# One-hots by head and operand in the start of an attention kernel, bf16 dummy products, and scaling and roundings moved to GpSimd

## The chip, the cores and the metric

The kernel runs on one core of a Trainium2 chip. The metric is the time of one execution in device microseconds; lower is better. In the text TensorE is the matrix engine (PE in the profile, PEld its weight loads), VectorE is DVE, ScalarE is ACT, GpSimd is POOL and SyncE is SP, whose queue issues the DMAs.

## The reference, cut to what matters

```
q_n, k_n, c_n = q / |q|, k / |k|, centroids / |centroids|
q_assign = argmax_c(q_n . c_n)          # 16 clusters a head
k_assign = argmax_c(k_n . c_n)
scores = where(q_assign == k_assign, q k^T / 8, -1e9)
attn = softmax(scores);  x = attn v      # 2 x 8 heads, 768 rows, width 64
x = leaky_relu(x @ w_in) @ w_out         # 1536 tokens, 512 -> 2048 -> 512
x = relu(x @ w2_in) ** 2 @ w2_out
```

## The kernel before, in words

The 16 heads stand in 8 pairs. A pair's q and k lie transposed in one tile `rqk` (128 partitions: two heads of width 64; `[:, 0]` is q, `[:, 1]` is k). Everything on the attention side is done in fp32 by splitting a number into a rounded part (type fp32r) and the rest: `hb` holds a head's q and k so split, and in 16 more rows of it the one-hots of the clusters, so that one product gives scores and mask together. For a pair that is prepared in the loop, `hi` and `lo` make the split parts in a tile `spl`, and DMAs place them in `hb`. The first pair is not placed by DMA: its q and k are loaded twice into tiles `twice` (SyncE's queue loads `cen`, the first pair's `rqk`, head 0's `twice`, the second pair's `rqk`, head 1's `twice`, then v), `head_hi` writes the rounded parts into `hb`, `head_lo` the rests (L579 for q, L584 for k, both on VectorE with two inputs in SBUF), `mask_mm` transposes the one-hots on TensorE, and `mask_act` writes them into `hb`.

At the start VectorE normalizes the centroids, TensorE transposes them (`ctp`), ScalarE copies them into the block matrix `cbd`, and 12 products (`dots`) give the first pair's dot products with the centroids, of k and then q. `is_max`, `rank`, `first_max` and `one_hot` turn them into one-hots in `pad`, for both heads and both operands at once. `warm_up` runs products of the identity whose result nobody reads.

The loop goes over units of two row tiles (128 rows of scores each); three units make a head. `PLAN` names the steps of a unit in order, each with the number of units by which it lags: S0, S1 scores (`qk_mm`), R0, R1 row maxima (`rowmax`), X0, X1 exponentials (`expo`), RE and RC row sums and reciprocals, N0, N1 normalization on GpSimd (`norm`), Ta to Tc transposes, H and L their rounded part and rest (`eh`, `el`), V the product with v. The order on every engine is the order in which this code is written; no scheduler changes it in this part. For the first units `hooks` hangs further work behind single steps: ("R1", 0) means behind the maximum of the second row tile of unit 0. There the second pair gets its dot products (`dots1`), its cluster maxima (`all_max1`), its ranks and one-hots (`rank`, `first_max`, `one_hot` on GpSimd and VectorE; `oh_trans` transposes them on TensorE), and head 1 gets its one-hots and its rests. GpSimd also splits v (`vlo`).

After the attention the two feed-forward layers follow, in fp32r products with weights split on ScalarE and GpSimd; the change does not touch them.

## Time and profile before

| | |
|---|---|
| time, median of 3 runs | 760.21 us (760.01 to 761.02) |
| time of the profiled execution | 760.79 us |
| its span, first to last instruction | 759.0 us |
| busy: TensorE, VectorE, ScalarE, GpSimd | 98%, 75%, 58%, 51% |
| granted TensorE clock, mean over the span | 0.998 |

A share of busy time is a mean over stages that differ: the start, in which TensorE waits for the other engines, is some 30 of 759 us. The first 30 us are the stretch that the change touches.

### The profile page before, as it was taken

The numbers are of one execution on the slowest core, as the hardware profiler recorded it, in microseconds if no ns is written. First come the engines' busy times: TensorE is split into PE (matmuls) and PEld (weight loads), VectorE is DVE, ScalarE is ACT, GpSimd is POOL, SyncE is SP. The second block draws the span as 40 slices with busy tenths as digits, with TensorE's granted clock in tenths as the row PEclk, the third lists the DMA queues.
The fourth block names the chain that finished last, engine by engine and source line by source line (L and its number), as shares of the span: only waits on it lengthen the run. The fifth ranks groups of instructions, "written<-read, shape, count | busy, mean of one in ns | idle before, by whom it ended". The sixth has DMA issues, their size and how long they took to land.

```text
span 759.0 us, 11071 instructions
## 1 busy us (share of the span) xinstructions
PE 745.1 (98%) x4054; PEld 649.5 (86%) x4054; DVE 570.8 (75%) x860; ACT 443.0 (58%) x816; POOL 387.4 (51%) x345
## 2 busy tenths in 40 slices
PE   8999999999999999999999999998999999999998
PEld 8899999999989888888888888887888888888886
DVE  5999999999999545876666576686568687687755
ACT  6988988988998564345444344556634444443430
POOL 2989889889855326561442414399242441424400
PEclk9999999999999999999999999999999999999999
DMA  7494574562601213111131112211111211122004
GB/s 231 102 220 110 118 172 111 116 173 68 156 21 62 107 56 111 55 56 57 56 111 56 55 56 73 94 57 56 56 57 62 99 62 55 56 76 91 1 1 166
DMA packets 16902, 66.35 MB, mean 87 GB/s; under 512 B 3152, under 2 KB 4048, under 8 KB 11856
## 3 DMA queue, kind: packets, MB, share of 16 engines
q1 hardware_dynamic: 16848, 65.65, 29.2%
q8 instruction: 32, 0.52, 0.3%
q14 instruction: 22, 0.18, 0.1%
HBM read 44.60 MB, written 3.15 MB: 63 GB/s over the span
## 4 chain that ended last, share of the span: by engine, by line
PE 85%; DVE 11%; ACT 3%; issue 1%; POOL 0%; DVEq 0%; POOLq 0%
PE o L847 35%; PE h L770 32%; PE A L487 6%; PE S L389 5%; PE T L452 5%; DVE el L469 4%; DVE nm L412 3%; ACT e L422 2%; ACT eh L463 1%; DVE ds L319 1%; DVE xt L509 1%; PE warm L242 1%; DVE m L318 1%; PE S L297 1%; DVE m L330 0%
## 5 line engine op out<-in xcount | busy, mean ns | idle before, releaser
L134 POOL TENSOR_TENSOR wl<-wt,wh 128x1024 fp32r<-128x1024 f32 x32 | 77.2, 2414 | 132.0 <-ACT wh L133 132.0
L818 DVE TENSOR_TENSOR gl<-h,gh 128x512 fp32r<-128x512 f32 x96 | 65.7, 690 | 69.0 <-ACT h L813 50.3
L770 PE MATMUL h<-xh,wh 128*128 128x512 f32 x288 | 112.0, 391 | 2.1 <-DVE gl L818 2.1
L770 PE MATMUL h<-xl,wh 128*128 128x512 f32 x288 | 112.5, 391 | 0.0
L770 PE MATMUL h<-xh,wl 128*128 128x512 f32 x288 | 112.2, 390 | 0.0
L865 DVE TENSOR_TENSOR acc<-o,acc 128x512 f32<-128x512 f32 x144 | 92.9, 686 | 12.4 <-PE o L847 12.4
L469 DVE TENSOR_TENSOR el<-T,eh 128x512 fp32r<-128x512 f32 x144 | 94.4, 683 | 4.4 <-ACT eh L463 3.2
L439 POOL TENSOR_SCALAR e<-e,r 128x768 f32<-128x768 f32 x96 | 87.6, 924 | 19.4 <-DVE r L436 13.1
L412 DVE TENSOR_REDUCE nm<-S 128x1 f32<-128x768 f32 x96 | 90.8, 947 | 4.2 <-PE S L297 2.4
L422 ACT ACTIVATE e<-S,nm 128x768 f32<-128x768 f32 x96 | 87.2, 909 | 11.1 <-DVE nm L412 6.7
L389 PE MATMUL S<-hb 128*128 128x384 f32 (+1 forms) x384 | 90.2, 349 | 2.0 <-ACT e L422 1.2
L463 ACT CAST eh<-T 128x512 fp32r<-128x512 f32 x144 | 79.9, 589 | 13.4 <-PE T L452 13.1
L487 PE MATMUL A<-eh,vv 128*128 128x256 f32 x288 | 79.6, 306 | 2.1 <-DVE xt L509 2.1
L452 PE MATMUL T<-ident,e 128*128 128x128 f32 x576 | 79.6, 273 | 1.0 <-DVE el L469 1.0
L847 PE MATMUL o<-wh,gh 128*128 128x512 f32 x192 | 75.2, 392 | 0.0
L197 POOL TENSOR_TENSOR ws<-wt 128x256 f32<-128x256 f32 x24 | 17.8, 741 | 112.4 <-DVE wt L173 112.4
L847 PE MATMUL o<-wl,gh 128*128 128x512 f32 x192 | 75.1, 391 | 0.0
L847 PE MATMUL o<-wh,gl 128*128 128x512 f32 x192 | 74.9, 390 | 0.0
L847 PE MATMUL o<-gl,wh 128*128 128x512 f32 x192 | 74.8, 390 | 0.0
L847 PE MATMUL o<-gh,wl 128*128 128x512 f32 x192 | 74.7, 389 | 0.0
L847 PE MATMUL o<-gh,wh 128*128 128x512 f32 x192 | 73.6, 389 | 0.0
L487 PE MATMUL A<-el,vv 128*128 128x256 f32 x288 | 72.5, 282 | 0.3 <-DVE el L469 0.3
(136 smaller groups left out, 1600.9 us busy)
## 6 DMA issues: line engine op xcount, KB each, us to landing
wraw<-w SPq DMA_DIRECT2D x32, 1024.0 KB, 4.7
hb<-spl SPq DMA_DIRECT2D x14, 576.0 KB, 4.7
hb<-spl SPq DMA_DIRECT2D x42, 192.0 KB, 5.2
rqk<-qk SPq DMA_DIRECT2D x16, 384.0 KB, 4.0
rv<-v SPq DMA_DIRECT2D x8, 384.0 KB, 3.3
out<-q SPq DMA_DIRECT2D x12, 256.0 KB, 2.0
twice<-qk SPq DMA_DIRECT2D x8, 192.0 KB, 5.8
hb<-st SPq DMA_DIRECT2D x56, 24.0 KB, 2.0
```

The costliest lines, as they stand in the source:

```text
L134: return lambda: nc.gpsimd.tensor_tensor(out=wl, in0=t, in1=wh.bitcast(F32), op=ALU.subtract)
L389: nc.tensor.matmul(out=s[:, c, 0:HALF], lhsT=hb[0:k, a, i * 128 : (i + 1) * 128], rhs=hb[0:k, b, c * HALF : (c + 1) * HALF], start=(a == 0 ...
L412: nc.vector.tensor_reduce(out=n, in_=s_t[t][:, :, 0:HALF], axis=AX.XY, op=ALU.max, negate=True)
L422: nc.scalar.activation(out=e.rearrange("p (a b) -> p a b", a=2), in_=s_t.pop(t)[:, :, 0:HALF], func=AF.Exp, bias=n_t.pop(t), scale=1.0, ac ...
L439: nc.gpsimd.tensor_scalar(out=e_t[t], in0=e_t[t], scalar1=r_t[t // 2][:, t % 2 : t % 2 + 1], scalar2=1.0, op0=ALU.mult, op1=ALU.mult,)
L452: nc.tensor.transpose(T[:, o : o + 128], e_t[2 * u + b][:, kc * 128 : (kc + 1) * 128], ident)
L463: nc.scalar.copy(out=eh[:, 2 * g : 2 * g + 2, :].rearrange("p a b -> p (a b)"), in_=T_t[u, g])
L469: nc.vector.tensor_tensor(out=el[:, 2 * g : 2 * g + 2, :].rearrange("p a b -> p (a b)"), in0=T_t.pop((u, g)), in1=eh[:, 2 * g : 2 * g + 2, ...
L487: nc.tensor.matmul(out=A, lhsT=w, rhs=m[:, kc, :], start=(kc == 0 and i == 0), stop=(kc == KC - 1 and i == 1),)
L770: nc.tensor.matmul(out=out, lhsT=l, rhs=r, start=(first and i == 0), stop=(i == n - 1), skip_group_check=not first,)
L847: nc.tensor.matmul(out=outs[o], lhsT=l, rhs=r, start=(first and i == 0), stop=(last and i == 2),)
L865: nc.vector.tensor_tensor(out=a, in0=ps, in1=a, op=ALU.add)
```

## The change

- The dummy products no longer use the identity. A tile `ones` (bf16, 128x512) is filled by VectorE's first instruction; `warm_up` multiplies it with itself, 512 or 128 columns wide, into the bank `tp1`, and stands at more places (9, 3, 5, 4 and 3 products in the start and the first unit, 8 short ones behind S1 of unit 1).
- The first pair's k is loaded ahead of its q. `dots` lies in another PSUM pool.
- The one-hots of the first pair are made by head and operand: `first_eq` (maximum and comparison) and `first_one` (rank, maximum, comparison), in the tiles `pad0` and `pad1`: head 0's k, its masks, then q, its masks; head 1 later.
- Head 0's third rounded copy, the second pair's scaling (`scale(1)`) and both its rounded parts (`hi(1, j)`) go from ScalarE to GpSimd. Head 0's rounded k on ScalarE moves behind the first two masks. One of the two copies into `cbd` goes from ScalarE to VectorE.
- The hooks of the first units are dealt out anew.

```diff
-FILL = (0,0,1)
+FILL = (8, 0, 8)
...
-    WARM = (9,4,10)
+    WARM = (9, 3, 5, 4, 3)
...
-    def warm_up(n):
-        w = ps_t.tile([128, 512], F32, tag="T", name="warm")
+    tp1 = ps_a.tile([128, 512], F32, tag="A", name="dots")
+    ones = ep.tile([128, S], F32, tag="e", name="ones")[:, 0:256].bitcast(BF16)
+
+    def warm_up(n, cols=512):
         for i in range(n):
-            nc.tensor.matmul(out=w[:, 0:128], lhsT=ident, rhs=ident, start=True, stop=True)
+            nc.tensor.matmul(
+                out=tp1[:, 512 - cols : 512], lhsT=ones[:, 0:128], rhs=ones[:, 0:cols],
+                start=True, stop=True,
+            )
...
-        nc.scalar.copy(out=cbd[64:128, :, C : 2 * C], in_=cview[:, :, 1])
+        nc.vector.tensor_copy(out=cbd[64:128, :, C : 2 * C], in_=cview[:, :, 1])
...
+    for j in (1, 0):
+        nc.sync.dma_start(out=rqks[0][:, j], in_=qk[0, j])
...
-            if h == 0:
-                nc.scalar.mul(out=o, in_=i, mul=scale)
...
+        if h == 0 and n < 2:
+            nc.scalar.mul(out=o, in_=i, mul=scale)
+        else:
+            nc.gpsimd.tensor_scalar(
+                out=o, in0=i, scalar1=scale, scalar2=1.0, op0=ALU.mult, op1=ALU.mult
+            )
...
-    warm_up(WARM[2])
-    head_hi(0)
-    nc.scalar.mul(out=rqks[1][:, 0], in_=rqks[1][:, 0], mul=0.125)
-    tp1 = ps_a.tile([128, 512], F32, tag="A", name="dots")
-    is_max(0, tp[:, 0 : 24 * C].rearrange("p (g c) -> p g c", c=C), slice(0, 24))
-    rank(0)
-    first_max(0)
-    one_hot(0)
-    head_lo(0, 0)
-    head_lo(0, 1)
...
+    def first_eq(h, j):
+        s = 6 * (1 - j)
+        d = tp[:, 0 : 24 * C].rearrange("p (t j h c) -> p j t h c", j=2, h=2, c=C)[:, j, :, h]
+        m = mfirst[:, 12 * h + s : 12 * h + s + 6]
+        x = pads[h][:, 4 + s : 10 + s]
+        mb = m.unsqueeze(2).to_broadcast([128, 6, C])
+        nc.vector.tensor_reduce(out=m, in_=d, axis=AX.X, op=ALU.max)
+        nc.vector.tensor_tensor(out=x, in0=d, in1=mb, op=ALU.is_equal)
+
+    def first_one(h, s, n):
+        m = mfirst[:, 12 * h + s : 12 * h + s + n]
+        x = pads[h][:, 4 + s : 4 + s + n]
+        mb = m.unsqueeze(2).to_broadcast([128, n, C])
+        nc.vector.tensor_tensor(out=x, in0=x, in1=desc[:, 0:n], op=ALU.mult)
+        nc.vector.tensor_reduce(out=m, in_=x, axis=AX.X, op=ALU.max)
+        nc.vector.tensor_tensor(out=x, in0=x, in1=mb, op=ALU.is_equal)
...
-    for i in range(4):
-        mask_mm(0, i)
-        mask_act(0, i)
-    spl[1] = splp.tile([128, 4, S], F32R, tag="spl", name="spl")
+    head_hi(0, 0)
+    head_hi(0, 2)
+    first_eq(0, 1)
+    first_one(0, 0, 6)
+    masks(0, 0, 1)
+    head_hi(0, 1)
+    warm_up(WARM[2])
+    first_eq(0, 0)
+    first_one(0, 6, 6)
+    head_lo(0, 0)
+    masks(0, 2, 3)
+    head_lo(0, 1)
+    first_eq(1, 1)
+    first_eq(1, 0)
+    warm_up(WARM[3])
+    scale(1)
     for j in (1, 0):
-        nc.scalar.copy(out=spl[1][:, j], in_=rqks[1][:, j])
-    head_hi(1)
+        hi(1, j)
+    for n in range(3):
+        head_hi(1, n)
...
-        ("S1", 0): [lambda: mask_mm(1, 0), lambda: mask_mm(1, 1), lambda: dots1(0, 6), lambda: warm_up(FILL[0])],
-        ("S0", 1): [lambda: dots1(6, 9), lambda: warm_up(FILL[1])],
-        ("S1", 1): [lambda: dots1(9, 12), lambda: mask_mm(1, 2), lambda: mask_mm(1, 3), lambda: warm_up(FILL[2])],
-        ("RE", 0): [lambda: recip(0), lambda: mask_act(1, 0), lambda: mask_act(1, 1), lambda: act_copy_v()],
-        ("R1", 0): [lambda: head_lo(1, 0), lambda: head_lo(1, 1)],
+        ("S1", 0): [lambda: warm_up(WARM[4]), lambda: dots1(0, 3)],
+        ("S0", 1): [lambda: dots1(3, 6)],
+        ("S1", 1): [
+            lambda: dots1(6, 9), lambda: mask_mm(1, 0), lambda: mask_mm(1, 1),
+            lambda: warm_up(FILL[0], 128),
+        ],
+        ("S0", 2): [lambda: dots1(9, 12), lambda: mask_mm(1, 2), lambda: mask_mm(1, 3)],
+        ("RE", 0): [lambda: recip(0), lambda: act_copy_v()],
+        ("R1", 0): [lambda: first_one(1, 0, 12)],
+        ("RE", 1): [lambda: mask_act(1, 0), lambda: mask_act(1, 1)],
+        ("X0", 2): [lambda: mask_act(1, 2), lambda: mask_act(1, 3)],
+        ("R1", 1): [lambda: head_lo(1, 0), lambda: head_lo(1, 1)],
+        ("R0", 2): [lambda: all_max1()],
...
-        ("R1", 1): [lambda: all_max1()],
-        ("RE", 1): [lambda: mask_act(1, 2), lambda: mask_act(1, 3)],
```

The order in which instructions stand on the engines shows where the pieces went. First VectorE, from the first cluster maximum to the first row maxima (`nm`); the brackets name whose semaphores a row waits for. Before:

```order
L318 TENSOR_REDUCE m<-dots 128x24 [waits PE_49]
L319 TENSOR_TENSOR pad<-dots,m 128x384 [waits DVE_49]
L324 TENSOR_TENSOR pad<-pad,desc 128x384 [waits DVE_49,Pool_49]
L330 TENSOR_REDUCE m_239<-pad 128x24 [waits DVE_49]
L335 TENSOR_TENSOR pad<-pad,m_239 128x384 [waits DVE_49]
L579 SCALAR_TENSOR_TENSOR hb<-twice,hb 64x768 [waits DMAHW4_49,Activation_49]
L584 TENSOR_TENSOR hb<-twice,hb 64x768 [waits DMAHW5_49,Activation_49]
L412 TENSOR_REDUCE nm<-S 128x1 [waits PE_49] x2
```

And in the change, up to the first operation on q's half and from its last one to the row maxima (L585 and L590 are the former L579 and L584, `pad_151` and `pad_153` are head 0's and head 1's one-hots):

```order
L609 TENSOR_REDUCE m<-dots 128x6 [waits PE_49]
L610 TENSOR_TENSOR pad_151<-dots,m 128x96 [waits DVE_49]
L616 TENSOR_TENSOR pad_151<-pad_151,desc 128x96 [waits DVE_49,Pool_49]
L617 TENSOR_REDUCE m<-pad_151 128x6 [waits DVE_49]
L618 TENSOR_TENSOR pad_151<-pad_151,m 128x96 [waits DVE_49]
L609 TENSOR_REDUCE m<-dots 128x6
...
L585 SCALAR_TENSOR_TENSOR hb<-twice,hb 64x768 [waits DMAHW4_49,Activation_49]
L590 TENSOR_TENSOR hb<-twice,hb 64x768 [waits DMAHW5_49,Activation_49]
L609 TENSOR_REDUCE m<-dots 128x6
L610 TENSOR_TENSOR pad_153<-dots,m 128x96 [waits DVE_49]
L609 TENSOR_REDUCE m<-dots 128x6
L610 TENSOR_TENSOR pad_153<-dots,m 128x96 [waits DVE_49]
L414 TENSOR_REDUCE nm<-S 128x1 [waits PE_49] x2
```

Five instructions of 384 elements became ten of 96 ahead of the two roundings, and four more stand behind them. Only the first of the reductions of `dots` waits for TensorE.

Second VectorE from the first row maxima to the sixth. Before:

```order
L412 TENSOR_REDUCE nm<-S 128x1 [waits PE_49] x2
L579 SCALAR_TENSOR_TENSOR hb<-twice,hb 64x768 [waits DMAHW2_49,Pool_49]
L584 TENSOR_TENSOR hb<-twice,hb 64x768 [waits DMAHW3_49,Pool_49]
L436 RECIPROCAL r<-r 128x2 [waits Activation_49]
L412 TENSOR_REDUCE nm<-S 128x1 [waits PE_49] x2
L318 TENSOR_REDUCE m<-dots 128x24 [waits PE_49]
L319 TENSOR_TENSOR ds<-dots,m 128x384 [waits DVE_49]
L412 TENSOR_REDUCE nm<-S 128x1 [waits PE_49]
L436 RECIPROCAL r<-r 128x2 [waits Activation_49]
L412 TENSOR_REDUCE nm<-S 128x1 [waits PE_49]
```

And in the change, behind the first two row maxima:

```order
L616 TENSOR_TENSOR pad_153<-pad_153,desc 128x192 [waits DVE_49]
L617 TENSOR_REDUCE m<-pad_153 128x12 [waits DVE_49]
L618 TENSOR_TENSOR pad_153<-pad_153,m 128x192 [waits DVE_49]
L438 RECIPROCAL r<-r 128x2 [waits Activation_49]
L414 TENSOR_REDUCE nm<-S 128x1 [waits PE_49] x2
L585 SCALAR_TENSOR_TENSOR hb<-twice,hb 64x768 [waits DMAHW2_49,Pool_49]
L590 TENSOR_TENSOR hb<-twice,hb 64x768 [waits DMAHW3_49,Pool_49]
L414 TENSOR_REDUCE nm<-S 128x1 [waits PE_49]
L323 TENSOR_REDUCE m<-dots 128x24 [waits DVE_49,PE_49]
L324 TENSOR_TENSOR ds<-dots,m 128x384 [waits DVE_49]
L438 RECIPROCAL r<-r 128x2 [waits Activation_49]
L414 TENSOR_REDUCE nm<-S 128x1 [waits PE_49]
```

Head 1's roundings moved from behind the second maximum to behind the fourth, and the second pair's cluster maxima from ahead of the fifth to behind it.

Third GpSimd, from its first work on loaded data to the second pair's one-hots (`oh`). Before:

```order
L570 TENSOR_SCALAR hb<-twice 128x768 [waits DMAHW2_49,DMAHW1_49]
L570 TENSOR_SCALAR hb<-twice 128x768 [waits DMAHW4_49,DMAHW3_49]
L570 TENSOR_SCALAR hb<-twice 64x768
L439 TENSOR_SCALAR e<-e,r 128x768 [waits DVE_49]
L439 TENSOR_SCALAR e<-e,r 128x768 [waits Activation_49]
L289 TENSOR_TENSOR vv<-rv,vv 128x6x128 [waits DMAHW5_49,Activation_49]
L324 TENSOR_TENSOR ds<-ds,desc 128x384 [waits DVE_49,Pool_49]
```

And in the change:

```order
L576 TENSOR_SCALAR hb<-twice 64x768 [waits DMAHW3_49]
L274 TENSOR_SCALAR rqk<-rqk 128x768 [waits DMAHW7_49]
L205 TENSOR_SCALAR spl<-rqk 128x768 [waits DMAHW0_49]
L205 TENSOR_SCALAR spl<-rqk 128x768 [waits Pool_49]
L576 TENSOR_SCALAR hb<-twice 128x768 [waits DMAHW2_49,DMAHW1_49]
L576 TENSOR_SCALAR hb<-twice 128x768 [waits DMAHW4_49,DMAHW3_49]
L576 TENSOR_SCALAR hb<-twice 64x768
L441 TENSOR_SCALAR e<-e,r 128x768 [waits DVE_49]
L441 TENSOR_SCALAR e<-e,r 128x768 [waits Activation_49]
L294 TENSOR_TENSOR vv<-rv,vv 128x6x128 [waits DMAHW5_49,Activation_49]
L329 TENSOR_TENSOR ds<-ds,desc 128x384 [waits DVE_49]
```

Four instructions came ahead of head 1's three copies; the rest of GpSimd's order is the same. On ScalarE the last two masks of head 1 stood ahead of the fifth exponential and stand behind it now.

## Rows read from the trace of the kernel before

**Rows 1.** The page, parts 1 and 4: busy time, and the chain by engine.

```profile
PE 745.1 (98%) x4054; PEld 649.5 (86%) x4054; DVE 570.8 (75%) x860; ACT 443.0 (58%) x816; POOL 387.4 (51%) x345
...
PE 85%; DVE 11%; ACT 3%; issue 1%; POOL 0%; DVEq 0%; POOLq 0%
```

**Rows 2.** The chain of waits to 60 us: start, us, engine, tile, line, count.

```profile
6.57 2.62 PE dots L297 x24
...
12.23 0.95 DVE hb L579
...
16.72 1.88 ACT e L422 x4
...
22.92 1.22 ACT hb L624 x2
...
24.16 0.99 ACT e L422 x2
...
28.89 0.33 PE ohT L350 x3
```

**Rows 3.** TensorE's timeline, 0 to 8 us: start, duration, line, operands, count.

```profile
1.40 4.16 PE L242 MATMUL warm<-ident 128*128 128x128 f32 x18 [1.40 <-POOL ident masks.py:199]
5.40 0.27 PE L262 MATMUL ctp<-ident,ct 128*64 128x128 f32 x1
5.51 1.06 PE L242 MATMUL warm<-ident 128*128 128x128 f32 x8
```

**Rows 4.** VectorE's timeline, from several stretches up to 44 us.

```profile
4.43 0.26 DVE L260 TENSOR_SCALAR ct<-ct,rn 128x64 f32<-128x64 f32 x1
...
9.20 0.56 DVE L318 TENSOR_REDUCE m<-dots 128x24 f32<-128x384 f32 x1 [4.51 <-PE dots L297]
...
13.22 1.55 DVE L584 TENSOR_TENSOR hb<-twice,hb 64x768 fp32r<-64x768 f32 x1
15.73 1.82 DVE L412 TENSOR_REDUCE nm<-S 128x1 f32<-128x768 f32 x2 [0.96 <-PE S L389]
...
18.57 0.95 DVE L584 TENSOR_TENSOR hb<-twice,hb 64x768 fp32r<-64x768 f32 x1
...
27.14 1.10 DVE L637 TENSOR_TENSOR spl<-rqk,spl 128x768 fp32r<-128x768 f32 x1
...
42.86 0.29 DVE L318 TENSOR_REDUCE m<-S 128x8 f32<-128x128 f32 x1 [0.53 <-ACT e L422]
```

**Rows 5.** GpSimd's timeline, 12.9 to 30 us.

```profile
13.14 0.83 POOL L570 TENSOR_SCALAR hb<-twice 128x768 fp32r<-128x768 f32 x1 [9.84 <-DMA twice<-qk]
14.72 1.64 POOL L570 TENSOR_SCALAR hb<-twice 128x768 fp32r<-128x768 f32 x2 [0.75 <-DMA twice<-qk]
19.70 1.80 POOL L439 TENSOR_SCALAR e<-e,r 128x768 f32<-128x768 f32 x2 [3.34 <-DVE r L436]
21.45 1.85 POOL L289 TENSOR_TENSOR vv<-rv,vv 128x768 fp32r<-128x768 f32 x1
23.24 1.02 POOL L324 TENSOR_TENSOR ds<-ds,desc 128x384 f32<-128x384 f32 x1
...
26.92 1.50 POOL L339 TENSOR_SCALAR oh<-ds 128x384 bf16<-128x384 f32 x1
```

**Rows 6.** ScalarE's timeline, 14 to 17 us.

```profile
15.00 1.58 ACT L633 CAST spl<-rqk 128x768 fp32r<-128x768 f32 x2
```

**Rows 7.** The second pair's q: issue on SyncE's queue; DMA view, us to landing.

```profile
4.61 0.59 SPq L233 DMA_DIRECT2D rqk<-qk  x1
...
rqk<-qk SPq DMA_DIRECT2D x1, 384.0 KB, 5.4
```

**Rows 8.** Between the two layers: TensorE's wait, then windows (PEclk ahead of DMA).

```profile
530.30 0.50 PE L770 MATMUL h<-xh,wh 128*128 128x512 f32 x1 [2.06 <-DVE gl L818]
...
531.00:532.00 1.00, 1.00 (x4) 0.72 (x3) 0.06 (x1) 1.00 (x4) 1.00 (x1) 0.52 0.00 0
...
534.00:535.00 1.00, 1.00 (x5) 0.76 (x5) 0.70 (x1) 0.23 (x2) 0.00 (x0) 0.77 0.00 0
```

51 lines of the change are left out of this document (25 added, 26 removed).

## The prediction

> **What bounds the kernel now.** First the page's busy shares and chain [rows 1]: TensorE is busy 98% of the span and makes 85% of the chain that ended last, so after the start almost nothing but its own work sets the time. Then the chain of waits over the first 30 us [rows 2]: there the chain does not lie on TensorE. It goes from the 12 cluster products (`dots`, 6.57, done 9.19) to VectorE, which writes one-hots and the two roundings of head 0 from 9.20 to 14.77, then to ScalarE from the first exponential at 16.72 almost without a break to the fifth at 24.16, and over VectorE at 28.89 to TensorE, on which it then mostly stays. The change moves instructions only ahead of this point. Behind it the order views of both kernels agree engine by engine, so what the point at 28.89 loses or wins should arrive at the end one for one. One place further back may be touched by a shift: at 531 us the granted clock falls to its lower level for some 3.4 us [rows 8]; it comes back below.
>
> **The start.** The dummy products wait for the identity until 1.40, and the 18 rows of the first nine end at 5.40, 0.22 us each; the next eight take 1.06 us, 0.13 each [rows 3]. The granted clock reads 1.00 throughout, but rows at half the rate are those of the lower level, 1.2 GHz. Now VectorE's first instruction fills the tile. No row has such a fill; VectorE's small instructions take 0.15 to 0.6 us, so the products begin between 0.9 and 1.3. A bf16 product of 512 columns has no row either: at the lower level [rows 8] show four products of 512 columns touched in a microsecond, so one takes a quarter to half a microsecond, and nine end between 3.2 and 5.8. The centroids' transpose goes then, but not before VectorE has its input (4.43 + 0.26, about 4.7 [rows 4]), against 5.40: between 0.7 us won and 0.4 lost. At 0.4 each from 1.3 they end at 4.9; I take 0.3 won. The second copy into `cbd` goes to VectorE, but the order view has it wait for ScalarE's copy, so they stay one behind the other: 0. The three short products behind lie beside these copies: 0 (0.2 to 0.3 without that cover).
>
> **Clusters by head and operand, k first.** Five instructions of 384 elements, 0.56 us each from 9.20, become ten of 96 for head 0 ahead of the roundings, and seven for head 1 later. 384 elements take 0.56 and 128 take 0.29 [rows 4], about 1.05 ns an element, so 96 take 0.26, about 0.30 with the gap: ten take 3.0 us, what the five took (9.20 to 12.23 [rows 2, 4]). That k comes first wins nothing, because the first reduction waits for all of `dots`: in the order view the second reduction, which reads q's, has no wait of its own. So head 0's roundings begin 3.0 us behind `dots`, as before. Head 1's four first instructions (1.2 us) now stand ahead of the first row maximum, where VectorE waited 0.96 us for scores [rows 4]: +0.25.
>
> **Scaling and roundings on GpSimd: the price.** ScalarE loses four instructions of 0.8 us and one copy. The two casts at 15.00 to 16.58 [rows 6] ended before the first exponential could start at 16.72, so that wins 0. GpSimd gets four of 0.83 us. The second pair's q lands at 10.0 (4.61 + 5.4 [rows 7]) and its k behind it, and head 1's three copies can go at 13.14 and 14.72 as before [rows 5]. So GpSimd, idle until 13.14 before, now has work that reads SBUF from 10.0 to 16.4 with short gaps, just while VectorE runs instructions with two SBUF inputs. The trace shows what that costs. The rounding L584 takes 0.95 alone at 18.57, but 1.55 at 13.22, with GpSimd's L570 from 13.14 to 13.97 [rows 4, 5]: it ends 0.80 after GpSimd does, as if it stood still until then. So each rounding that finds GpSimd at work loses about 0.6, and GpSimd's next one waits in turn. If nothing collides, head 0's roundings end 3.0 + 2 x 0.97 = 4.95 after `dots`, against 5.6 now: with the start 0.95 us earlier. If both roundings and two one-hot steps collide (0.6, 0.6, 0.6, 0.4) they end 1.25 later. Both roundings fall where GpSimd has work queued, the one-hot steps mostly before: I take 1.25 us of collisions, +0.3; with the 0.25 above the first exponential is some **0.6 later** (bounds -0.9 and +1.5, and the start's own).
>
> A page speaks to this. The Trainium skill's "SBUF — State Buffer", section "Who interferes with whom", says that VectorE with two SBUF inputs and a GpSimd instruction that reads SBUF exclude each other for the whole instruction. L584 agrees; L637 at 27.14 does not: it runs inside GpSimd's cast L339 (26.92 to 28.42) and takes 1.10, not the 2.1 that this rule would give [rows 4, 5]. By the rule the sum below would be 1.0 higher; it goes by the rows.
>
> **Head 1's roundings, moved back.** Call x the end of the second exponential (18.60 [rows 2]). Before, the two roundings were done at 19.52 (the second from 18.57 [rows 4]), while GpSimd was idle until 19.70 [rows 5]. Now they stand behind the fourth row maximum. VectorE: reciprocal x+0.5, two maxima to x+2.2, then the roundings. GpSimd: two normalizations of 0.9 from x+0.6 to x+2.4, then the split of v, 1.85 us [rows 5]. The first rounding waits to x+2.4 and ends x+3.2; the split, queued behind, takes the memory to x+4.95; the second rounding ends 0.80 later, x+5.75. The fifth maximum, queued behind it, ends x+6.7, and the fifth exponential x+7.7; before it ended at 25.15, x+6.55 [rows 2]. **+1.15**. If both roundings got in first, the maximum would end x+5.0 and the exponential x+6.0: -0.55.
>
> **Head 1's last masks.** Two mask writes, 1.22 us [rows 2], ran ahead of the fifth exponential, and now run behind it, ahead of `eh` and the sixth. The time ahead of it is now spent waiting for the maximum, so they are paid in full: **+1.2** (0.8 if the sixth maximum is late anyway).
>
> **The second pair's one-hots.** VectorE's cluster maxima of pair 1 (two instructions of 0.56) stood ahead of the fifth maximum and now follow it: done x+7.8. GpSimd needs 5.2 us from there, as from 23.24 to 28.42 [rows 5]: x+13.0, or x+13.8 when VectorE's rounding L637 (now L669) gets in between. TensorE's transposes of them, behind which everything queues, stood at 28.89 = x+10.3; with the two terms above they would stand at x+12.65. **+0.35 to +1.3**, I take 0.9.
>
> The dummy products in the middle (five, four, three long ones, eight short) lie where TensorE waits for VectorE or ScalarE: 0; without that cover the four cost about 0.9, the others 0.5 each.
>
> **Sum.** 0.6 + 1.15 + 1.2 + 0.9 = 3.85 us. The profiled execution took 760.79 with a span of 759.0, so by it 764.6; it lies 0.6 over the median of the runs, so from 760.21 I predict **764.0**.
>
> **Rivals.** (a) Not slower: head 1's second rounding is issued before GpSimd's split of v begins. That decides from about 1 us: if GpSimd's two normalizations end after x+3.2, that term turns to -0.55, the last falls to 0.3, the masks cost 0.8 to 1.2, and with the first scores between -0.9 and +0.6 the sum is about +0.6: 760.8. For it: the margin is a microsecond in a chain that I only estimate. Against: the split stood directly behind the normalizations (19.70 and 21.45 [rows 5]) and still does. (b) Faster: as (a), with no collision at head 0, and the seam: after a wait of 2.06 us TensorE runs at the lower level in four microseconds that lack 0.48, 0.50, 0.50 and 0.23 of the clock, 1.7 us in all [rows 8]. A shifted program might not meet the fall: 760.8 - 0.9 - 1.7 = 758.2. Nothing in a single trace says that it will. (c) GpSimd's cast holds L669 to its end, as that page has it for every such pair. From rows: 28.42 + 0.80 = 29.2 against 28.24, so 1.0 more: 765.0. L637's own row speaks against it. (d) The first reduction does not wait for q's products: VectorE starts 1.3 earlier, 762.7; the missing wait in the order view speaks against it.
>
> **How the numbers follow.** Chances: forecast 0.5, (c) 0.08, (d) 0.04, (a) 0.26, (b) 0.12. The forecast's own range is 762.4 to 765.8, from the bounds of its terms taken partly together. The range of all reaches down into (a), leaves out (b): 759.6 to 766.0. Within 0.2% is 1.5 us, about what a measurement here can tell from no change. Faster 0.12, from (b). Same 0.26, from (a). Slower 0.62.
>
> **What would show it.** Right: both roundings of head 0 and the second of head 1 last 1.5 us or more, each ending 0.8 after a GpSimd instruction; ScalarE idle before the fifth exponential; TensorE idle before the one-hot transposes. Wrong: roundings of 0.95 us, ScalarE busy without a break from the first exponential, or the same order further back giving lost time back.

## The result, and the profile after

| | before | after |
|---|---|---|
| time, median of 5 runs each | 760.21 us (760.01 to 761.06) | 767.68 us (766.27 to 769.32) |
| ratio, 95% interval | | 1.0093 (1.0081 to 1.0105) |
| span of the profiled execution | 759.0 us | 765.9 us |

Slower by 7.5 us, where 764.0 (3.8 us slower) with a range of 759.6 to 766.0 was forecast: the direction was right, the forecast size half of what came.

The page of the changed kernel, parts 1 and 4, reads almost as before [rows 1]; five more microseconds of TensorE's time count as busy, with 16 instructions fewer. Busy time grows like that when the same rows take longer; the dummies, now wider, add to it (their rows sum to 9.5 us, before to 8.1).

```profile
PE 750.4 (98%) x4038; PEld 649.5 (85%) x4038; DVE 576.9 (75%) x874; ACT 439.8 (57%) x811; POOL 392.1 (51%) x350
...
PE 85%; DVE 10%; ACT 3%; issue 1%; DVEq 0%; ACTq 0%
```

The chain of waits to 60 us (start, us, engine, tile, line, count), to be read beside [rows 2]:

```profile
6.28 2.88 PE dots L302 x24
10.43 0.61 DVE pad L618
11.17 1.47 PE ohT L629 x6
12.64 2.13 PE dots L244 x5
14.77 1.28 PE ohT L629 x6
16.05 0.97 PE dots L244 x4
17.02 0.72 PE S L391 x4
17.77 0.97 DVE nm L414
18.76 1.00 ACT e L424 x2
...
23.20 2.48 DVE hb L585
25.70 0.95 DVE hb L590
26.65 0.88 DVE nm L414
27.55 0.99 ACT e L424 x2
28.57 1.22 ACT hb L638 x2
...
31.46 1.65 PE S L391 x4
33.11 1.71 PE T L454 x8
```

Two things stand in it. The middle part (23.20 to 29.79) is what the prediction described: a rounding of head 1 behind GpSimd, the maximum behind it, the exponential, the masks. But the first part is TensorE's, and dummy products (`dots` of L244) are links of the chain, where the prediction had VectorE's roundings.

Four marks divide the loss. They are ends and starts of rows in both timelines: the second exponential's end (18.51, now 20.54), the fifth's (25.06, now 28.45), the start of the second pair's one-hot transposes (28.89, now 34.61), the fiftieth exponential's end (131.15, now 137.76).

| stretch | longer by | forecast |
|---|---|---|
| to the second exponential | 2.03 | 0.6 |
| from there to the fifth | 1.36 | 1.15 |
| from there to the one-hot transposes | 2.33 | 1.2 + 0.9 |
| from there to the fiftieth exponential | 0.89 | 0 |
| from there to the end | 0.25 | 0 |
| sum | 6.86 | 3.85 |

The two middle terms came within 0.25 us each. The first and the fourth did not, and both have the same neighbour: the granted clock. Windows of the changed kernel (PEclk stands ahead of the DMA share), where before it read 1.00:

```profile
9.00:10.00 1.00, 0.14 (x2) 0.03 (x1) 0.67 (x3) 0.00 (x0) 0.00 (x0) 0.66 1.05 424
10.00:11.00 1.00, 0.00 (x0) 0.00 (x0) 0.93 (x4) 0.00 (x0) 0.83 (x1) 0.50 1.10 323
...
16.00:17.00 1.00, 1.00 (x6) 0.52 (x4) 0.97 (x4) 0.75 (x2) 1.00 (x1) 0.93 0.47 187
...
29.00:30.00 1.00, 0.75 (x4) 0.63 (x4) 0.82 (x2) 0.98 (x3) 1.00 (x2) 0.90 0.00 0
30.00:31.00 1.00, 1.00 (x5) 0.65 (x3) 0.81 (x2) 0.97 (x2) 1.00 (x2) 0.50 0.00 0
...
36.00:37.00 1.00, 1.00 (x6) 0.97 (x6) 0.65 (x2) 1.00 (x3) 1.00 (x3) 0.69 0.73 147
```

0.66 over the microsecond from 9 is a fall at 9.3, 0.93 over that from 16 a rise at 16.1; in the same way the second stretch at 0.50 (1.2 GHz) reaches from 29.8 to 36.6. The first fall lies only some 0.15 us behind the end of the dots (9.16), so the length of the wait that begins there cannot have brought it; what work in that place does is tried below. TensorE's timeline shows the wait, and the rows at the lower level:

```profile
11.17 1.47 PE L629 MATMUL ohT<-ident,pad 128*80 128x128 f32 x6 [2.02 <-DVE pad L618]
12.43 2.34 PE L244 MATMUL dots<-ones 128*128 128x512 bf16 x5
14.56 1.49 PE L629 MATMUL ohT<-ident,pad 128*80 128x128 f32 x6
15.85 1.18 PE L244 MATMUL dots<-ones 128*128 128x512 bf16 x4
```

Behind the dots TensorE waited 2.02 us, where the kernel before ran ten dummies. Then five bf16 dummies took 2.34 us and held q's masks, and four more held the first scores until 16.67. Before, 12 transposes took 1.58; here two lots of six take 1.47 and 1.49.

VectorE was late as well. Its timeline:

```profile
10.43 0.60 DVE L618 TENSOR_TENSOR pad<-pad,m 128x96 f32<-128x96 f32 x1
...
11.52 0.93 DVE L616 TENSOR_TENSOR pad<-pad,desc 128x96 f32<-128x96 f32 x1
...
12.77 0.47 DVE L618 TENSOR_TENSOR pad<-pad,m 128x96 f32<-128x96 f32 x1
13.27 1.46 DVE L585 SCALAR_TENSOR_TENSOR hb<-twice,hb 64x768 fp32r<-64x768 f32 x1
14.77 1.61 DVE L590 TENSOR_TENSOR hb<-twice,hb 64x768 fp32r<-64x768 f32 x1
...
17.77 1.82 DVE L414 TENSOR_REDUCE nm<-S 128x1 f32<-128x768 f32 x2 [0.47 <-PE S L391]
...
23.20 2.47 DVE L585 SCALAR_TENSOR_TENSOR hb<-twice,hb 64x768 fp32r<-64x768 f32 x1
```

The other seven instructions of 96 elements took 0.24 to 0.26. So these three lost 0.34, 0.67 and 0.21, and head 0's roundings 0.51 and 0.66 against 0.95: 2.4 us of collisions, not 1.25. The roundings end at 16.38, 1.6 later than before. With head 1's four instructions behind them VectorE was free for the first maximum at 17.30, 1.57 later than it started before, and waited another 0.47 for TensorE's scores.

Head 1's rounding of 2.47 met GpSimd's split of v, as the prediction had it, but it is the first of the two that was held, not the second:

```profile
23.02 1.83 POOL L294 TENSOR_TENSOR vv<-rv,vv 128x768 fp32r<-128x768 f32 x1
...
32.31 2.08 POOL L341 TENSOR_SCALAR oh<-ds 128x384 bf16<-128x384 f32 x1
```

The split ended at 24.85 and the rounding 0.82 later, the rule seen at L584 [rows 4, 5]. By the Trainium skill's "SBUF — State Buffer", section "Who interferes with whom", whoever issues first keeps the shared pair of SBUF ports for the whole instruction; both rows agree, for the cast L341 this time stood still behind VectorE's L669 (31.90 to 33.03) and took 2.08 instead of 1.50. It was done at 34.39, 13.8 behind the second exponential as put. TensorE began the transposes of these one-hots at 34.61 without a wait in front of them, because its rows from 31.46 on ran at the lower level (the eight transposes `T` in 1.91 us, before in 1.04):

```profile
34.61 0.53 PE L352 MATMUL ohT<-identb,oh 128*128 128x128 bf16 x3
```

So of the third stretch at most 0.2 us is the clock's; the rest is GpSimd's path.

### The profile page after: what moved, and what is told of

It is laid out like the page before. It is cut to its first block, busy times and chain, and to the rows that moved or that the text cites. A ratio compares the mean times of both kernels' runs of the same rounds, so it can differ in the third digit from the quotient of the medians.

```text
span 765.9 us, 11056 instructions
## 1 busy us (share of the span) xinstructions
PE 750.4 (98%) x4038; PEld 649.5 (85%) x4038; DVE 576.9 (75%) x874; ACT 439.8 (57%) x811; POOL 392.1 (51%) x350
## 4 chain that ended last, share of the span: by engine, by line
PE 85%; DVE 10%; ACT 3%; issue 1%; DVEq 0%; ACTq 0%
PE o L885 34%; PE h L808 32%; PE A L489 6%; PE S L391 6%; PE T L454 5%; DVE el L471 3%; DVE nm L414 3%; ACT e L424 2%; PE dots L244 1%; ACT eh L465 1%; DVE xt L511 1%; DVE ds L324 1%; PE S L302 1%; DVE m L323 1%; PE dots L302 0%
## 5 line engine op out<-in xcount | busy, mean ns | idle before, releaser
L465 ACT CAST eh<-T 128x512 fp32r<-128x512 f32 x144 | 79.7, 588 | 13.1 <-PE T L454 12.9
L197 POOL TENSOR_TENSOR ws<-wt 128x256 f32<-128x256 f32 x24 | 17.8, 741 | 112.5 <-DVE wt L173 112.5
L454 PEld LDWEIGHTS T<-ident,e 128*128 128x128 f32 x576 | 70.1, 145 | 4.1 <-POOL e L441 1.3
```

The lines of the kernel that those rows point to most:

```text
L454: nc.tensor.transpose(T[:, o : o + 128], e_t[2 * u + b][:, kc * 128 : (kc + 1) * 128], ident)
L465: nc.scalar.copy(out=eh[:, 2 * g : 2 * g + 2, :].rearrange("p a b -> p (a b)"), in_=T_t[u, g])
```

## The theories and the experiments

**Theory "order"**: the time is set by the order on VectorE and GpSimd, as the prediction had it, only with more collisions. **Theory "clock and dummies"**: the first and last terms come from TensorE. The change takes the dummies out of one wait and puts long ones ahead of masks and scores; the waits bring the clock down, and the rows behind run at half the rate.

All runs in one table. The time is a median; the ratio is to the kernel before on the same chip (its medians there 760.1 to 760.8). The last two columns come from the profiled execution: the end of the second exponential, and from there to the one-hot transposes (18.51 and 10.38 before, 20.54 and 14.07 in the changed kernel).

| kernel | time, us | ratio, 95% | 2nd exp. | to transposes |
|---|---|---|---|---|
| e1_fill: changed, gap behind dots filled | 768.69 | 1.0076 to 1.0130 | 19.91 | 14.07 |
| e2_round: changed, head 1's roundings early | 764.55 | 1.0038 to 1.0078 | 22.64 | 12.97 |
| e3_act: changed, second pair on ScalarE | 768.31 | 1.0079 to 1.0121 | 22.38 | 14.06 |
| e4_hooks: changed, three hooks put back | 765.61 | 1.0037 to 1.0082 | 20.59 | 12.53 |
| a1_old: changed, dummies of before | 766.93 | 1.0078 to 1.0109 | 19.15 | 15.17 |
| a2_all: a1_old, e3_act, e4_hooks together | 766.83 | 1.0068 to 1.0094 | 19.66 | 15.59 |
| f1_closed: e1_fill and e4_hooks together | 764.58 | 1.0040 to 1.0066 | 19.37 | 12.56 |
| b1_dummies: before, the change's dummies alone | 764.22 | 1.0049 to 1.0074 | 21.39 | 11.28 |
| c1_fill: b1_dummies, gap filled | 763.43 | 1.0023 to 1.0046 | 19.25 | 11.30 |
| f2_ident: c1_fill, first groups of identity | 761.31 | 1.0003 to 1.0025 | 20.05 | 11.29 |
| b2_pool: before, GpSimd's moves alone | 761.90 | 1.0003 to 1.0024 | 19.30 | 10.37 |
| c2_hooks: before, the hooks alone | 764.91 | 1.0044 to 1.0070 | 18.56 | 15.77 |
| f3_hooks_fed: c2_hooks, first waits filled | 764.73 | 1.0039 to 1.0065 | 18.88 | 13.95 |
| best1: before, dots in two tiles | 759.68 | 0.9985 to 1.0005 | 17.40 | 10.89 |
| best1_again: the same | 759.14 | 0.9967 to 0.9989 | 17.17 | 11.97 |
| best2: best1, dummies dealt anew | 760.48 | 0.9999 to 1.0016 | 17.02 | 11.26 |
| best3: best1, head 1's copies reordered | 759.66 | 0.9971 to 0.9992 | 17.85 | 10.39 |

### One part of the change undone

**The gap behind the dots filled.**

```diff
     all_dots(0, tp, slice(0, 2 * KC))
+    warm_up(8)
```

> The changed kernel (767.7) with eight more dummy products of 512 columns behind the first pair's 24 dots rows, where TensorE waited 2.02 us and the granted clock then read 0.5 from 9.3 to 16.1 us. Theory 'order' (VectorE's and GpSimd's instructions set the start): VectorE's roundings still end at 16.4, the first exponential comes 0 to 0.4 earlier, 767.2 to 767.7, and the second stretch at 0.5 (from 29.8) stays. Theory 'clock' (the lower level is what the change costs): the first stretch at 0.5 is gone, the masks and first scores come 1 us or more earlier, 766.7 or less. If the dummies end behind the first masks' one-hots (over 11.2 us) they cost instead.

In the profiled execution (765.71) the clock stayed up to 30.2 and the second exponential came 0.63 earlier: more than "order" allowed, less than "clock" asked, because now the roundings held (16.05). The other three executions took 768.5 to 770.2, with a mean granted clock of 0.991 to 0.993 against 0.996, so the edit does not help the time; where their clock was low no trace shows. Inconclusive by itself.

**Head 1's roundings early.**

```diff
-        ("R1", 0): [lambda: first_one(1, 0, 12)],
+        ("R1", 0): [lambda: head_lo(1, 0), lambda: head_lo(1, 1), lambda: first_one(1, 0, 12)],
-        ("R1", 1): [lambda: head_lo(1, 0), lambda: head_lo(1, 1)],
```

> The changed kernel with head 1's two roundings back behind the second row maximum, ahead of head 1's ranks; nothing else. Theory 'order': GpSimd is idle there until 21.3, so both take 0.95 us; the fifth maximum and exponential come 1.15 to 1.4 earlier, 766.3 to 766.6; if TensorE's wait at 27.0 to 28.6 shrinks so far that the second stretch at 0.5 does not come, another 1.2 less, 765.2. Theory 'clock' alone: no change while TensorE's waits stay, 767.7; the two differ by the time of the fifth exponential (27.55 in the changed kernel).

The mechanism came as expected: the roundings took 0.95 each, the fifth exponential came 7.06 behind the second instead of 7.91, and the second fall did not come in the profiled execution. The sizes did not: 0.85 us there instead of 1.15 to 1.4, and 3.1 by the medians, more than "order" asked. The profile is of the slowest of the four executions (766.33; the others took 764.0 to 765.0), and its start went worse. TensorE's timeline shows it; the same 24 rows of the dots took 2.76 in the kernel before and 2.87 in the changed kernel:

```profile
6.28 5.33 PE L302 MATMUL dots<-cbd,rqk 128*128 128x32 f32 x24 [0.29 <-DVE cbd L270]
```

Up to there the program is that of the changed kernel. So the lower level at the start lasts longer in one execution than in another. The mean granted clock does not show this: it reads 1.000 for this execution, and the windows read 1.00 over the dots. The Trainium skill's "TensorE: Matmul & The Clock Gate", section "Part 1: The HAM clock gate", says that the point of the rise varies from run to run of one kernel; these two traces agree, by 2.5 us on 24 rows.

**The second pair back on ScalarE.**

```diff
+    spl[1] = splp.tile([128, 4, S], F32R, tag="spl", name="spl")
+    nc.scalar.mul(out=rqks[1][:, 0], in_=rqks[1][:, 0], mul=0.125)
+    nc.scalar.copy(out=spl[1][:, 0], in_=rqks[1][:, 0])
...
+    nc.scalar.copy(out=spl[1][:, 1], in_=rqks[1][:, 1])
-    scale(1)
-    for j in (1, 0):
-        hi(1, j)
```

> The changed kernel with the second pair's scaling and two rounded copies back on ScalarE (in its idle time between head 0's copies and masks), GpSimd keeping head 1's three copies. Theory 'collisions' (VectorE's two-input instructions stand still behind GpSimd's): VectorE's third, eighth and tenth one-hot instructions fall from 0.60, 0.93 and 0.47 us to 0.26 each, at least one rounding from 1.5 to 0.95; head 0's roundings end 1.2 to 2.3 earlier than 16.4 and the time falls to 765.4 to 766.5. Rival: the masks and the scores on TensorE at the lower clock set the first exponential, then less than 0.5 us comes of it, 767.2 or more.

The three one-hot instructions did fall to 0.26, 0.35 and 0.26, but both roundings still took 1.61 and 1.46, now behind head 1's copies, and the time did not fall. The profiled execution again had its dots in 5.33 us, so its second exponential (22.38) cannot be compared. The time is what the rival expected, but it settles little: the edit took away the one-hots' collisions (about 1.1 us) and left those of the roundings.

**Three hooks put back.**

```diff
-        ("S0", 2): [lambda: dots1(9, 12), lambda: mask_mm(1, 2), lambda: mask_mm(1, 3)],
+        ("S0", 2): [lambda: dots1(9, 12), lambda: mask_mm(1, 2), lambda: mask_mm(1, 3), lambda: all_max1()],
-        ("R1", 0): [lambda: first_one(1, 0, 12)],
-        ("RE", 1): [lambda: mask_act(1, 0), lambda: mask_act(1, 1)],
-        ("X0", 2): [lambda: mask_act(1, 2), lambda: mask_act(1, 3)],
-        ("R1", 1): [lambda: head_lo(1, 0), lambda: head_lo(1, 1)],
-        ("R0", 2): [lambda: all_max1()],
+        ("R1", 0): [lambda: head_lo(1, 0), lambda: head_lo(1, 1), lambda: first_one(1, 0, 12)],
+        ("RE", 1): [lambda: mask_act(1, 0), lambda: mask_act(1, 1), lambda: mask_act(1, 2), lambda: mask_act(1, 3)],
```

> The changed kernel with the hooks of the first units as before in three respects: head 1's roundings behind the second row maximum, its last two masks ahead of the fifth exponential, the second pair's cluster maxima ahead of the fifth row maximum. Theory 'order': the three terms of the prediction come back (1.15 + 1.2 + 0.35 to 1.3), 764.1 to 765.0, and with the second stretch at 0.5 gone 763 to 764. Rival 'clock': only that stretch matters and only if it goes, 766.5.

2.1 us back, less than expected: the second pair's dots and head 1's masks still stand a unit later than before, and VectorE waits 1.81 us for them. But its start tells the two theories apart. Here VectorE's instructions came first and GpSimd's copies second, and VectorE's timeline has next to no collision (one of the ten one-hot instructions took 0.39):

```profile
12.19 0.95 DVE L585 SCALAR_TENSOR_TENSOR hb<-twice,hb 64x768 fp32r<-64x768 f32 x1
13.72 0.95 DVE L590 TENSOR_TENSOR hb<-twice,hb 64x768 fp32r<-64x768 f32 x1 [0.58 <-ACT hb L574]
...
17.82 1.82 DVE L414 TENSOR_REDUCE nm<-S 128x1 f32<-128x768 f32 x2 [2.23 <-PE S L391]
```

The roundings are done at 14.67, as in the kernel before, and yet the first maximum waits 2.23 us for TensorE and starts where it does in the changed kernel (17.77). TensorE alone, with its clock (0.50 from 9.8 to 16.6) and its dummies, set the first scores.

**The dummies of before in the changed kernel** (ten behind the dots, none in the middle, one in the first units), and then **this with the hooks above and ScalarE's work put back**.

```diff
-FILL = (8, 0, 8)
+FILL = (0,0,1)
-    WARM = (9, 3, 5, 4, 3)
+    WARM = (9,4,10)
...
+            nc.tensor.matmul(out=w[:, 0:128], lhsT=ident, rhs=ident, start=True, stop=True)
...
     all_dots(0, tp, slice(0, 2 * KC))
+    warm_up(WARM[2])
...
-    warm_up(WARM[2])
...
-    warm_up(WARM[3])
```

> The changed kernel with the dummy products of the kernel before: products of the identity, 9 + 4, ten behind the dots, one in the first unit. Theory 'clock and dummies': the clock rises once, near 5.4 to 6.3, and stays up; the first row maximum stands 0.6 to 1.0 behind the last rounding; about 1.5 less for the start and 1.1 less behind the one-hot transposes if the second stretch at 0.5 goes too: 765 to 766.3, spread below 1.5 us. Theory 'order': the roundings at 16.4 set the start with or without them, 767.2 to 767.7.

> The changed kernel with the dummy products, the hooks (roundings, masks, cluster maxima) and the second pair's GpSimd work put back, so that the first pair's order by head and operand with k first is most of what is left. If ten instructions of 96 take what five of 384 took, head 0's roundings end at 14.6 to 14.9 and the first exponential lies within 0.4 of 16.7: 760.2 to 761.0. If the four instructions of head 1 ahead of the first maximum and the later ranks of head 1 cost (head 1's masks then wait for them), 761.5 to 763, and a fall of the clock in TensorE's waits adds 1 or more.

Both missed, and they say most. In a1_old's profiled execution, the fastest of its four (764.89), the start came back (second exponential 19.15) but the gain went again: with fewer dots and no masks ahead, and no dummies, TensorE waited 0.50 and 0.71 us between 13 and 15, and the clock was at 0.50 from 15.9 to 26.2. TensorE's timeline:

```profile
14.91 2.32 PE L387 MATMUL S<-hb 80*128 80x384 f32 x7 [0.71 <-DVE hb L585]
17.02 1.32 PE L298 MATMUL dots<-cbd,rqk 128*128 128x32 f32 x6
```

Six rows of the dots take 1.32 us instead of 0.75, and VectorE waits for scores again and again (0.60, 1.60, 1.12 us). In a2_all the clock was low from 15.1 to 32.2. So three of four parts undone won next to nothing (766.83 against 767.68), each time with a new long stretch at the lower level. In the changed kernel the clock was up from 16.1 to 29.8; that its later dummies keep it up there is likely, but no run takes out these alone.

**Both waits closed** (e1_fill's and e4_hooks' edits).

> The changed kernel with both of TensorE's long waits closed: eight more dummy products behind the dots (as in the run that kept the clock up to 30 us), and head 1's roundings, its last masks and the second pair's cluster maxima back where the kernel before has them. Theory 'waits bring the clock down': no stretch at 0.5 between 6 and 40 us in the profile; second exponential near 19.9, one-hot transposes 12.5 later at 32.4, so 762.5 to 763.7 where the clock rises early, 765 or more in executions where it rises late. Theory 'order alone': 763.8 to 765.6 as with the hooks put back alone, whatever the clock does.

In the profile no fall came behind 12.1, but one did at 8.7, while the dots ran, 2.6 us behind a wait of 0.44. Row and window:

```profile
6.16 3.03 PE L302 MATMUL dots<-cbd,rqk 128*128 128x32 f32 x24 [0.44 <-DVE cbd L270]
```

```profile
8.00:9.00 1.00, 1.00 (x10) 1.00 (x10) 0.00 (x0) 0.48 (x1) 0.00 (x0) 0.86 0.99 261
```

Up to there the program is that of e1_fill, whose clock stayed up. So dummies behind the dots do not rule a fall out; here it lasted 3.4 us, where without them it lasted 6.8 (the changed kernel, e4_hooks, and b1_dummies below). The time, 764.58, lies where "order" had it. With both undone the change still costs 3.8 us.

### One part done alone in the kernel before

**The dummies alone.** WARM, FILL, the bf16 tile and `warm_up` as in the change, also the three and the eight dummies behind S1 of the first two units; for the other places:

```diff
-    warm_up(WARM[2])
     head_hi(0)
...
         mask_mm(0, i)
         mask_act(0, i)
+        if i % 2:
+            warm_up(WARM[2 + i // 2])
```

> The kernel before with the change's dummy products alone: bf16 products from the tile filled by VectorE, 9 + 3 ahead of the dots, none behind them, 5 behind the first two masks, 4 ahead of the first scores, 3 and 8 in the first unit; all else as before. Theory 'clock and dummies' (they are most of what the first scores lose): TensorE waits some 3 us behind the dots, the granted clock falls there or rises late, the masks and scores wait behind dummies of 0.43 us, first exponential 1 to 3 later than 16.72; 761.5 to 763.5, with a larger spread. Theory 'order' (VectorE and GpSimd set the start, the prediction's): dummies lie in TensorE's waits, 759.9 to 760.7.

4.1 us, four of five runs between 763.97 and 764.62: "clock and dummies", above its range. VectorE and GpSimd do what they did before; the clock was at 0.50 from 9.8 to 16.6. TensorE's timeline, and one row of VectorE's:

```profile
12.36 1.48 PE L619 MATMUL ohT<-ident,pad 128*80 128x128 f32 x6 [3.18 <-DVE pad L340]
13.63 2.34 PE L244 MATMUL dots<-ones 128*128 128x512 bf16 x5
15.76 1.26 PE L619 MATMUL ohT<-ident,pad 128*80 128x128 f32 x6
```

```profile
18.61 1.82 DVE L417 TENSOR_REDUCE nm<-S 128x1 f32<-128x768 f32 x2 [3.92 <-PE S L394]
```

The first maximum waits 3.92 us for scores, where it waited 0.96 [rows 4].

**The gap filled in it, and then the first groups of identity products.**

```diff
     all_dots(0, tp, slice(0, 2 * KC))
+    warm_up(10)
...
-    warm_up(WARM[0])
+    warm_id(9)
-    warm_up(WARM[1], 128)
+    warm_id(4)
```

> The kernel before with the change's dummy products alone (764.2 measured), plus ten more of 512 columns behind the dots, where TensorE then waited 3.18 us and the granted clock fell to 0.5 from 9.82 to 16.65. Theory 'the wait behind the dots brings the fall, and the fall makes the dummies and masks long': the clock stays at 1.0, the masks of q end near 14.5 instead of 17.9, first exponential near 17.0; 760.2 to 761.2. Rival 'the dummies' place costs' (five ahead of q's masks, four ahead of the scores, whatever the clock): still 762 or more.

> The kernel before with the change's later dummy products and ten behind the dots, but the first two groups (9 and 4) as before, products of the identity in fp32. The same with bf16 in the first groups spread from 761.0 to 765.4. Theory 'the first bf16 dummies let the clock rise late in some executions': the spread shrinks to that of the kernel before, 760.6 to 762.0, median 761.2. Rival: the spread comes from the later dummies and waits, then it stays above 3 us with a median of 762.5 or more.

With ten dummies behind the dots the profile of c1_fill has no fall ahead of 760 us, and the second exponential comes at 19.25 instead of 21.39: the empty stretch and the fall in it go together, and cost 2.1 of 2.9 us there. The rest, 0.74, is the dummies' place. The time did not follow: its median, 763.43, is what the rival expected, and it spread from 761.0 to 765.4; the profiled execution (762.26) was one of the faster ones. With identity products ahead of the dots the median fell to 761.31; eight of twelve runs lie at 760.4 to 761.3, but four at 763.2 to 763.5, so the spread shrank only to 3.1 us. The first groups are part of it, not all. Against the kernel before, by medians, the dummies cost 4.1 us as the change has them, 2.9 with the gap filled, and 0.6 when the first groups are identity products too: the middle ones in their places are cheap, and most of the price lies in the gap and in the first groups.

**GpSimd's moves alone.**

```diff
-    nc.scalar.mul(out=rqks[1][:, 0], in_=rqks[1][:, 0], mul=0.125)
-        nc.scalar.copy(out=spl[1][:, j], in_=rqks[1][:, j])
+    scale(1)
+        hi(1, j)
```

> The kernel before with the change's moves to GpSimd alone: head 0's third rounded copy, the second pair's scaling and its two rounded copies. Theory 'collisions': two or three of VectorE's one-hot instructions of 384 elements and both of head 0's roundings stand still behind GpSimd's, 0.3 to 0.65 each; head 0's roundings end 0.5 to 1.3 later than 14.77 and the time is 760.7 to 761.5. Rival: ScalarE's 4.0 us less of work lets the first exponential start as soon as the row maximum is there, and nothing is lost: 759.8 to 760.3.

Collisions, as expected: VectorE's rows of 384 elements took 0.92 and 0.70 instead of 0.56, the roundings as here, and ended 0.8 later, at 15.57. It arrives at the end: 1.1 us by the ratio (1.0014), 1.8 by the medians (761.90 against 760.13).

```profile
12.62 1.47 DVE L579 SCALAR_TENSOR_TENSOR hb<-twice,hb 64x768 fp32r<-64x768 f32 x1
14.11 1.46 DVE L584 TENSOR_TENSOR hb<-twice,hb 64x768 fp32r<-64x768 f32 x1
```

**The hooks alone, and then with the first waits filled.** The change's table of hooks without its dummies and `first_one`; then

```diff
-        ("S1", 0): [lambda: dots1(0, 3)],
+        ("S1", 0): [lambda: dots1(0, 3), lambda: warm_up(4)],
-        ("S0", 2): [lambda: dots1(9, 12), lambda: mask_mm(1, 2), lambda: mask_mm(1, 3)],
+        ("S0", 2): [lambda: dots1(9, 12), lambda: mask_mm(1, 2), lambda: mask_mm(1, 3), lambda: warm_up(4)],
```

> The kernel before with the change's hooks alone: head 1's roundings behind the fourth row maximum, its masks ahead of and behind the fifth exponential, the second pair's cluster maxima behind the fifth maximum, its dots and head 1's transposes where the change has them. Theory 'order' (three terms of the prediction): the second exponential ends as before (18.5), the fifth 1.1 to 1.4 later (26.2 to 26.5), the one-hot transposes 3.2 to 3.7 later (32.1 to 32.6); 763.4 to 764.0, or up to 765 where the longer waits of TensorE bring a fall of the clock. Rival: TensorE has slack later and takes some back, 761.5 or less.

> The kernel before with the change's hooks alone (764.9 measured; the granted clock was 0.5 from 17.97 to 31.62), plus four dummy products of the identity behind the first dots of the second pair, where TensorE then waited 0.78 us, and four behind head 1's last transposes. Theory 'order': without the fall the fifth exponential ends 7.9 behind the second and the one-hot transposes 13.5 to 14 behind it (32.0 to 32.6), 763.4 to 764.0. Theory 'clock': most of the 4.3 us was the fall, transposes within 2 of 28.9, 761 to 762.

Both near 764.8, by two mechanisms. In c2_hooks TensorE ran out of work in the first unit, waited 0.78 us, and the clock fell from 18.0 to 31.6; its timeline, every row of the later units at half the rate:

```profile
17.82 1.54 PE L389 MATMUL S<-hb 128*128 128x384 f32 x4 [0.78 <-ACT e L422]
19.16 1.32 PE L297 MATMUL dots<-cbd,rqk 128*128 128x32 f32 x6
```

In f3_hooks_fed the clock stayed up to 30.3, and the order alone did it up to the fifth exponential: head 1's rounding met the split of v as in the changed kernel, and the fifth exponential came 7.89 behind the second (7.91 there). The transposes came 13.95 behind it (14.07 there); the clock was at 0.50 from 30.3 to 33.7 then, but GpSimd's one-hots were done only 0.06 us before them.

```profile
21.51 2.47 DVE L579 SCALAR_TENSOR_TENSOR hb<-twice,hb 64x768 fp32r<-64x768 f32 x1
24.02 0.95 DVE L584 TENSOR_TENSOR hb<-twice,hb 64x768 fp32r<-64x768 f32 x1
```

In c2_hooks, TensorE being late, the roundings began at 22.95, when the split (21.03, 1.81 us) was done, and took 0.96 and 0.95. The two losses hide each other.

### A version that is a little faster

The change loads k first, but its first reduction waits for all of `dots`. With k's and q's dots in two PSUM tiles it need not:

```diff
-    tp = ps_t.tile([128, 512], F32, tag="T", name="dots")
-    all_dots(0, tp, slice(0, 2 * KC))
+    tps = {j: ps_s.tile([128, 2, 512], F32, tag="S", name="dots")[:, 0] for j in (1, 0)}
+    for j in (1, 0):
+        for t in range(KC):
+            dot(0, t, j, tps[j][:, t * 2 * C : (t + 1) * 2 * C])
...
+    for j in (1, 0):
+        s = 12 * (1 - j)
+        d = tps[j][:, 0 : 12 * C].rearrange("p (g c) -> p g c", c=C)
```

with the five one-hot instructions of 192 elements for k, then for q, both heads together.

> The kernel before with what 'k first' could have meant: the first pair's dots of k and of q in two PSUM tiles, and the five one-hot instructions done for k (192 elements) while TensorE still makes q's, then for q. VectorE's first reduction then waits for k's products only, 1.3 us earlier than 9.20; one-hots end near 11.4 instead of 12.23, the roundings start 0.8 earlier and the second misses GpSimd's copy at 13.14, so they end near 13.4 instead of 14.77. If that arrives at the end, 758.8 to 759.4; if ScalarE's masks and casts (to 16.58 before) hold the first exponential, 759.8 to 760.3.

> The version with k's and q's dots in two PSUM tiles once more, beside the one above on the same chip: 0.3 to 0.8 less than the kernel before if its 1.1 us at the first exponential and 0.6 at the one-hot transposes arrive at the end.

VectorE's timeline of the second of these runs:

```profile
7.52 0.36 DVE L609 TENSOR_REDUCE m<-dots 128x12 f32<-128x192 f32 x1 [2.76 <-PE dots L297]
...
11.38 0.96 DVE L579 SCALAR_TENSOR_TENSOR hb<-twice,hb 64x768 fp32r<-64x768 f32 x1
12.37 0.95 DVE L584 TENSOR_TENSOR hb<-twice,hb 64x768 fp32r<-64x768 f32 x1
14.27 1.82 DVE L412 TENSOR_REDUCE nm<-S 128x1 f32<-128x768 f32 x2 [0.95 <-PE S L389]
```

The first reduction starts at 7.52 instead of 9.20, the second rounding misses GpSimd's copy, and the first maximum starts at 14.27 instead of 15.73. Part of it is lost again at head 1's roundings, which wait for GpSimd's copies of late loads. The first time it could not be told from the kernel before, the second time it was 1.4 us faster (0.9967 to 0.9989): at most some 0.2%, and clear of the noise in one of the two.

Two edits on top of it:

```diff
-    WARM = (9,4,10)
+    WARM = (8,4,3)
...
+        if i == 1:
+            warm_up(5)
+            nc.scalar.mul(out=rqks[1][:, 0], in_=rqks[1][:, 0], mul=0.125)
```

> The version with k's and q's dots in two PSUM tiles (759.7 measured) with one dummy product less ahead of the centroids' transpose (8), three dummies behind the dots instead of ten, k's masks ahead of five more dummies, and the second pair's scaling on ScalarE behind k's masks. k's masks then go at 9.5 instead of 11.0, q's at 11.4; the roundings at 13.3 set the scores alone: first exponential 0.3 to 0.8 earlier, 758.9 to 759.4. If the shorter dummies let the clock fall, 761 or more.

```diff
+        if h == 1:
+            parts = [parts[0], parts[2], parts[1]]
```

> The version with k's and q's dots in two PSUM tiles (759.7 against 760.1) with one more edit: GpSimd makes head 1's third copy (from q) ahead of the one from k, whose load lands last, so that it works on q while k is still on its way. In the version without it the copies ran to 18.13 and VectorE's two roundings of head 1 took 1.27 and 1.46 us; now they should be done near 18.4 instead of 18.94, the third row maximum 0.4 to 0.5 earlier, 759.2 to 759.6. If the loads land early anyway, no change: 759.5 to 760.1.

Dealing the dummies anew won 0.4 at the second exponential and nothing at the transposes (28.28 against 28.29), and the time was that of the kernel before. With head 1's copies reordered its roundings took 0.95 each and the transposes stood at 28.24; 0.9982 (0.9971 to 0.9992), the same as without it.

## Why the prediction was wrong

**The step that failed** is "The dummy products in the middle (five, four, three long ones, eight short) lie where TensorE waits for VectorE or ScalarE: 0". The dummies alone cost 4.1 us in the kernel before. Two things were missed in it. The ten dummies that the change takes from behind the dots were not priced: in the three profiled executions with that place left empty and an early rise (waits of 2.02, 1.68 and 3.18 us) the granted clock fell to 0.50, 0.2 to 0.6 us into the wait, and stayed there for 6.8 us. What brings the fall is not shown beyond that; with bf16 dummies there, three of four had none. And a dummy in a wait is free only if it is done when the wait is; at half the rate five of them took 2.34 us and stood ahead of q's masks. Where the gap is filled and the first groups are identity products, the middle ones cost 0.6 us (f2_ident), so the 0 was not far off for their places; what it left out is the clock. The price at no cover (0.9 and 0.5) was worked out at the upper rate and from the wrong cover. The seam's fall [rows 8] was quoted as a place where a shift might win, not read as something that can stand behind a wait of TensorE.

**The collisions** were the second miss, a size: 2.4 us instead of 1.25 in the profiled execution. By themselves they make the first maximum 1.57 later, where the first term had 0.6. The 0.3 that the bf16 dummies at the start were to win did not come either: nine of them took 4.02 us from 1.44, and the first reduction starts at 9.18, before at 9.20. That the first reduction waits for q, that ten instructions of 96 take what five of 384 took (9.20 to 12.16 in e4_hooks, where next to nothing met GpSimd), and that k first wins nothing came as put. For the first exponential the two misses don't add, since either chain alone makes it late: with the dummies it stays where it was when the collisions are gone (e4_hooks), and with the clock up it wins 0.63 until VectorE holds (e1_fill).

**Head 1's roundings, masks and the one-hots** went as put in order and size: 1.36 for 1.15, 2.33 for 2.1. Two details differ: the first rounding was held instead of the second, and TensorE was not idle ahead of the one-hot transposes, since its clock was low. Rival (a) would have needed the second rounding issued ahead of the split; even the first came 0.18 us behind the split's start. Rival (c) did not come about: the cast met L669, but L669 was first and the cast waited.

**That the start arrives one for one** held, up to the clock: from the transposes to the fiftieth exponential the kernel before took 102.26 and every kernel whose clock was up there 102.2 to 102.6. The changed kernel took 103.15, with TensorE at the lower level for the first 2.0 us of it (34.61 to 36.6), and e1_fill 103.61, with 3.1 us.

**The seam**, of rival (b), is a matter of the execution and not of the program: from the fiftieth exponential to the end the same kernel took 627.88 (best1) and 626.36 (best1_again), with a fall at 530 and without. Two others without one took 627.7 and 628.2, so the fall is not all that varies there.

Left open: what the clock did in executions without a profile, so how much of the changed kernel's spread of 3 us is a late rise; and what share of the 7.5 us belongs to each part, since parts hide each other (alone they cost 4.1, 1.1 and 4.3). The fourth part, the first pair's one-hots by head and operand, was never run alone with the clock up; a2_all, which was to show it, met a fall of its own.

## What to carry to other kernels

Before filling work is taken out of a wait of TensorE, or work is moved so that TensorE waits, read what the granted clock does behind the waits that are there already, and price the rows behind a fall at up to twice their length (six rows of the dots took 1.32 us instead of 0.75). Where VectorE and GpSimd share a stretch, look at which of them will issue first: a rounding that started 0.18 us behind GpSimd's split took 2.47 us, the one behind it 0.95. And when an operand is to come first, give it a tile of its own, or the first consumer waits for both.
